# Activation tables set for single steps at the start of a feed-forward stage, and the first weight conversion behind the first activations

## The chip, the cores and the metric

The kernel runs on one core of one Trainium2 chip. The time is the device time of one execution in microseconds (us); lower is better. Five engines work side by side, each through its own queue in order: TensorE (PE in the profile; its weight loads are PEld), VectorE (DVE), ScalarE (ACT), GpSimd (POOL) and SyncE (SP, which here only issues DMAs).

## The reference, cut to what matters

Three blocks follow each other: attention with a compressive memory, a dense feed-forward block, and a layer of eight experts with routing. The change is in the second:

```
h  = x @ w_in                      # 2304 x 512  by 512 x 2048
sp = log1p(exp(min(h, 20)))        # h itself where h > 20
g  = h * tanh(sp)                  # Mish
y  = g @ w_out                     # 2304 x 2048 by 2048 x 512
```

The third block routes by the largest logit of y, so the kernel keeps products near full precision: each operand is split into a high part, rounded to the fp32r type of the matmuls, and the rest, and three products (high x high, low x high, high x low) are summed.

## The kernel before, in words

The tokens are cut into 9 blocks of 256 (`NBLK`), the 2048 hidden columns into 8 pairs of 128 (`STEPS`). A step is one block and one pair; there are 72, and `order` lists them: the first blocks 0 and 1 by turns, then block after block. So step 0 is block 0, pair 0; step 1 is block 1, pair 0; step 2 is block 0, pair 1.

For a step s there are these functions, and no planner: in this stage the order in which the program emits instructions is the order of every queue.

- `gemm1(s)`: 24 matmuls into a PSUM tile `ph`, of which there are three, so `gemm1(s + 3)` waits until ACT has read the tile of s.
- `mish_a(s)`: on ACT, Silu into g (L209) and a Tanh into t (L210). They belong to one activation table (`SILU`).
- `mish_b(s)`: Mish is finished with Arctan (L220) and Sin (L221), which lie in another table (`TRIG`). It does nothing for an even step; for an odd step it changes the table (L217), does Arctan and Sin for the steps s - 1 and s, and changes back (L222). DVE then does one operation per step (L225), `g = (t + c) * g`.
- `mish_d(s)`: splits g for the second product: on DVE a cast to gh (L232) and a subtraction to gl (L235).
- `gemm2(s)`: 12 matmuls that add the step into the sums `py` (L249 to L251). They read gh, gl and the steps' rows of `w_out`, both parts. Of three matmuls the first two read gh, the third gl.
- `convert(s)`: `w_out` arrives as float64 words and is converted while the first 16 steps run. A call does the high part of row block s on ACT (L834, tile u), the low part on POOL (L837), three bit operations for row block s + 1 on DVE (L813, L818, L824, which `cv.bits` issues), one load by SP (L792), and the scaling of row block s + 2 on ACT (L805). The high part of s needs the bit operations of s, issued by the call before.

The loop over s (L598) emits: `gemm1(s)`, `mish_a(s)`, `mish_d(s - 2)`, `mish_b(s)`, `convert(s + 1)` while there are rows left, and `gemm2(s - 3)` from s = 3 on. `convert(0)` stands ahead of the loop, with the bit operations of row block 1 in it; the bit operations of row block 0 are done during attention. `xs.load(2)` at s = 0 loads a block of tokens that attention stored.

The converted `w_out` tiles u lie in memory that attention used, so the first write to them waits until attention has ended, its last product on POOL (L1146) included. The tiles g, t, gh and gl are in other pools, opened later, in memory that attention's input tiles used.

Of the kernel before, what the change touches and what calls it, by code (L numbers as in the profile page):

```python
# [43 lines left out]
def fused_kernel(ctx, tc, qk, qn, vx, beta, w_in, w_out, wgs, wgk, w1, w2, out, dbg=None):  # L44
# [26 lines left out]
    more = ctx.enter_context(tc.tile_pool(name="more", bufs=1))  # L71
    uw += [more.tile([128, 4096], F32R, name=f"u{i}") for i in range(4, 8)]
    moe(tc, wgs, wgk, w1, w2, out, yd, rt, ident, shift, right, uw, xs, cv)
    if "xd" in dbg:
        for b in range(B):
# [33 lines left out]
def moe(tc, wgs, wgk, w1, w2, out, yd, rt, ident, shift, right, uw, xs, cv):  # L109
# [5 lines left out]
    with ExitStack() as ctx:  # L115
# [22 lines left out]
        def wo_parts(f):  # L138
            sl = slice((f % 8) * 512, (f % 8 + 1) * 512)
            return uw[4 + f // 8][:, sl], uw[6 + f // 8][:, sl]  # L140
# [17 lines left out]
        def tables():  # L158
            SP.dma_start(out=wgt, in_=wgk)
            G.iota(c8, [[-1, NE]], base=NE, channel_multiplier=0, allow_small_or_imprecise_dtypes=True)  # L160
            G.iota(tok, [[128, NTILE]], base=0, channel_multiplier=1)
            G.iota(spread, [[0, 1]], base=0, channel_multiplier=16, allow_small_or_imprecise_dtypes=True)
            V.memset(ones, 1.0)
            G.affine_select(out=tri, in_=ones, pattern=[[1, 128]], compare_op=ALU.is_gt, fill=0.0, base=0, channel_multiplier=-1)
            V.memset(cum, 0.0)
            V.memset(empty[:, :, 0:1], OOB)
            V.memset(empty[:, :, 1:2], 0)
            for e in range(NE):
                for t in range(2):
                    SP.dma_start(out=rtv[t][:, e], in_=empty)  # L170
            SP.dma_start(out=yd[N:N + 1, :].rearrange("a (p c) -> (a p) c", p=128), in_=ident[:, 0:4])

        def rows():
            for e in range(NE + 1):
                if e % 2 == 0 and e < 6:
                    pair = cv.pool.tile([128, 2, DM], F32, name="raw", bufs=cv.bufs[0])
                if e < 6:
                    row = pair[:, e % 2]
                else:
                    row = cv.pool.tile([128, DM], F32, name="cvt" if e < 8 else "cvf", bufs=2)  # L180
                SP.dma_start(out=row, in_=wgs[e:e + 1].to_broadcast([128, DM]))
                wrows.append(row)
            wrows.append(cv.pool.tile([128, DM], F32, name="cvf", bufs=2))
# [28 lines left out]

        def mish_b(s):

            if s % 2 == 0:
                return
            nc.scalar.preload_act_table_set(TRIG)  # L217
            for x in (s - 1, s):
                g, t = gs[x]
                A.activation(out=t, in_=t, func=AF.Arctan, scale=TAN8)  # L220
                A.activation(out=t, in_=t, func=AF.Sin, scale=2.0, bias=right)  # L221
            nc.scalar.preload_act_table_set(SILU)  # L222
            for x in (s - 1, s):
                g, t = gs[x]
                V.scalar_tensor_tensor(out=g, in0=t, scalar=ROOT_HALF, in1=g, op0=ALU.add, op1=ALU.mult)  # L225

        def mish_d(s):
            g, t = gs[s]
            gh = gp.tile([128, 2, TOK], F32R, name="gh")
            gl = gp.tile([128, 2, TOK], F32R, name="gl")  # L230
            if s < KF:
                V.tensor_copy(out=gh, in_=g)  # L232
            else:
                A.activation(out=gh, in_=g, func=AF.Copy)  # L234
            V.tensor_tensor(out=gl, in0=g, in1=gh.bitcast(F32), op=ALU.subtract)  # L235
            gs[s] = (gh, gl)
# [198 lines left out]
        def load_w(q=SP):  # L435
            tag = next((x for x in room if room[x]), None)
            if at[0] >= stop[0] or tag is None:
                return
            room[tag] -= 1
            r, m, c = chunks[at[0]]  # L440
            at[0] += 1
            rows = slice(c * 128 * (m + 1), (c + 1) * 128 * (m + 1))
            src = (w1, w2)[m][bass.ds(first_e[0], 1) if r == 0 else slice(r - 1, r), rows].rearrange("a p f -> (a p) f")
            pool = cv.pool if tag == "raw" else xs.pool
            raw = pool.tile([128, KD, TOK], F32, name=tag, bufs=size[tag]).rearrange("p a b -> p (a b)")
            if m == 0:
                q.dma_start(out=raw, in_=src)
            else:
                q.dma_start(out=raw.rearrange("p (k f) -> p k f", k=2),
                            in_=src.rearrange("(k p) f -> p k f", p=128))  # L450
            raws[r, m, c] = (raw, tag)
# [122 lines left out]
        def first_block(b):  # L574
            return stages(0, (ga, gb)[b]["first"], (ta, tb)[b]["first"], id0[:, b, 0:1], id0[:, b, 1:2].bitcast(F32))
# [6 lines left out]
        def convert(s):  # L582
            if s < KF:
                cv.high(s, *wo_parts(s))
                cv.low(s, *wo_parts(s))
            if s + 1 < KF:
                cv.bits(s + 1)
            if s + cv.ahead < KF:
                cv.load_out(s + cv.ahead)
            if s + 2 < KF:  # L590
                cv.scale(s + 2)

        def on(f, s):
            if 0 <= s < total:
                f(s)

        convert(0)
        for s in range(total + GLAG):  # L598
            i, j = order[s] if s < total else (NBLK, s - total)
            if s == 0:  # L600
                xs.load(2)
            if 2 <= i < NBLK - 1 and j == 0:
                xs.load(i + 1)
            on(gemm1, s)
            on(mish_a, s)
            on(mish_d, s - 2)
            on(mish_b, s)
            if s == 2 * STEPS - 2:
                for k in range(KD):
                    xs.split(2, k)  # L610
            if s + 1 < KF:
                convert(s + 1)
            if s == KF - 1:
                rows()
            if s == 6:
                tables()
            if 2 <= i < NBLK - 1 and 3 <= j < 3 + KD:
                xs.split(i + 1, j - 3)
            if s == total - STEPS:
                for _ in range(3):  # L620
                    load_w()
            if s == total - STEPS + 3:
                room["raw"] = 3
                for _ in range(3):
                    load_w()
            if s >= GLAG:
                b, jb = order[s - GLAG]
                gemm2(s - GLAG)
                if jb == STEPS - 1:
                    for n in (2 * b, 2 * b + 1):  # L630
                        store_y(n)
                if s == total:
                    first = first_block(0)
                    next(first)
                    first_gather(1)
                for q in tail_splits.get(s, ()):
                    split_w(q)
                if jb == STEPS - 1:
                    if b < NBLK - 1:
                        two_b = (2 * b, 2 * b + 1)  # L640
                        if b < 2 or b == NBLK - 2:
                            group = [[(logits, n) for n in two_b], [(logits2, n) for n in two_b], [(route_a, b)]]
                            if b == NBLK - 2:
                                for g, f in zip(group, ((fill_first,), (), (first_gather,))):
                                    g[:0] = [f] * bool(f)
                            todo += [[]] * (b == 0) + group
                        else:
                            flat = [(logit, n, e) for n in two_b for e in range(NE + 1)]
                            group = [flat[x:x + 3] for x in range(0, len(flat), 3)]
                            if b == NBLK - 3:  # L650
                                group[0][:0] = [(pick_first,)]
                            todo += group + [[(route_a, b)]]
                        if b == NBLK - 2:
                            todo += [[(turn_a, "first")], [(route_b, b)], [(route_c, b)]]
                        else:
                            todo += [[(route_b, b)], [(route_c, b)]]
            last = None
            while todo and (last is None or last is logit and todo[0][0][0] is route_a):
                last = 0
                for it in todo.pop(0):  # L660
                    it[0](*it[1:])
                    last = it[0]
# [177 lines left out]
class Work:  # L840
# [59 lines left out]
    on = {}  # L900
# [415 lines left out]
```

## Time and profile before

| | |
|---|---|
| median of three runs | 899.84 us (898.0 to 900.85) |
| the profiled execution | 903.65 us, its span 901.9 us |
| PE busy | 844.4 us, 94% of the span |
| ACT busy | 622.4 us, 69% |
| DVE busy | 577.8 us, 64% |
| POOL busy | 278.4 us, 31% |
| mean granted clock of TensorE | 0.978 of full speed |

The stage of the change begins at 235.26 us of the span, with the first matmul of `gemm1(0)`. Times in the rows below are counted from the span's start. In a timeline a row is one instruction: start, duration, engine, line, operation, what it writes and reads, and in brackets how long the engine sat idle before it and what ended that.

### The profile page before, as it was taken

The numbers are of one execution on the slowest core, as the hardware profiler recorded it, in microseconds if no ns is written. First come the engines' busy times: TensorE is split into PE (matmuls) and PEld (weight loads), VectorE is DVE, ScalarE is ACT, GpSimd is POOL, SyncE is SP. The second block draws the span as 40 slices with busy tenths as digits, with TensorE's granted clock in tenths as the row PEclk, the third lists the DMA queues.
The fourth block names the chain that finished last, engine by engine and source line by source line (L and its number), as shares of the span: only waits on it lengthen the run. The fifth ranks groups of instructions, "written<-read, shape, count | busy, mean of one in ns | idle before, by whom it ended". The sixth has DMA issues, their size and how long they took to land.

```text
span 901.9 us, 15116 instructions
## 1 busy us (share of the span) xinstructions
PE 844.4 (94%) x5412; PEld 687.3 (76%) x5412; DVE 577.8 (64%) x1171; ACT 622.4 (69%) x1136; POOL 278.4 (31%) x358
## 2 busy tenths in 40 slices
PE   5899999999889999999999999999988989989995
PEld 3566656666779998989898989888866867768774
DVE  6988878766488843356575757575558666373661
ACT  4687768876588887787878788787845555363551
POOL 5876776854223230110111111011103212211200
PEclk8999999999999999999999999999989999999998
DMA  6666657642333231010101010122336958284610
GB/s 211 192 197 206 200 168 230 214 143 87 123 94 110 94 129 49 24 47 24 48 24 48 25 48 24 48 94 95 95 125 211 349 197 288 67 288 151 198 62 4
DMA packets 53704, 113.44 MB, mean 126 GB/s; under 512 B 12148, under 2 KB 17396, under 8 KB 53600
## 3 DMA queue, kind: packets, MB, share of 16 engines
q1 hardware_dynamic: 43968, 91.22, 31.3%
q0 software_dynamic: 4064, 10.42, 3.5%
q10 hardware_dynamic: 5568, 10.49, 3.2%
q8 instruction: 56, 0.92, 0.4%
q14 instruction: 48, 0.39, 0.1%
HBM read 94.47 MB, written 18.77 MB: 126 GB/s over the span
## 4 chain that ended last, share of the span: by engine, by line
PE 40%; DMA 21%; issue 15%; ACT 8%; POOL 7%; DVE 5%; SPq 1%; ACTq 0%; POOLq 0%; another core or an unknown queue 0%; DVEq 0%
DMA cvt<-yd,ids 8%; DMA out<-cvf,ids 6%; PE ph L197 6%; PE ph L199 6%; PE ph L198 6%; PE py L249 6%; PE py L251 6%; PE py L250 6%; DMA r<-rd 3%; DMA qn<-qn 2%; PE px L1134 2%; PE pt L1106 2%; POOL mn L1027 1%; ACT e L1074 1%; DVE nm L1063 1%
## 5 line engine op out<-in xcount | busy, mean ns | idle before, releaser
L197 PE MATMUL ph<-xh,u 128*128 128x256 f32 x576 | 163.8, 284 | 0.9 <-DVE xr L1006 0.9
L199 PE MATMUL ph<-xh,u 128*128 128x256 f32 x576 | 162.5, 282 | 0.0
L198 PE MATMUL ph<-xl,u 128*128 128x256 f32 x576 | 162.3, 282 | 0.0
L249 PE MATMUL py<-u,gh 128*128 128x512 f32 x288 | 115.8, 402 | 4.9 <-POOL u L837 4.9
L251 PE MATMUL py<-u,gl 128*128 128x512 f32 x288 | 115.7, 402 | 4.2 <-DVE gl L235 4.2
L250 PE MATMUL py<-u,gh 128*128 128x512 f32 x288 | 115.1, 400 | 0.0
L197 PEld LDWEIGHTS ph<-xh,u 128*128 128x128 f32 x576 | 109.8, 191 | 3.4 <-DVE xr L1006 1.1
L198 PEld LDWEIGHTS ph<-xl,u 128*128 128x128 f32 x576 | 109.8, 191 | 2.5
L199 PEld LDWEIGHTS ph<-xh,u 128*128 128x128 f32 x576 | 109.8, 191 | 0.0
L225 DVE SCALAR_TENSOR_TENSOR g<-t,g 128x512 f32<-128x512 f32 x72 | 49.9, 693 | 92.0 <-ACT t L221 89.8
L1074 ACT ACTIVATE e<-ps,nm 128x256 f32<-128x256 f32 (+4 forms) x144 | 78.0, 550 | 29.7 <-DVE nm L1063 21.9
L235 DVE TENSOR_TENSOR gl<-g,gh 128x512 fp32r<-128x512 f32 x72 | 51.1, 709 | 62.4 <-ACT gh L234 53.9
L1106 PE MATMUL pt<-ident,e 128*128 128x128 f32 x528 | 77.0, 285 | 8.3 <-ACT eta L1008 5.6
L351 POOL DMA_INDIRECT rt<-pay,sl x18 | 22.1, 1225 | 181.6 <-DVE pay L349 178.8
L209 ACT ACTIVATE g<-ph 128x512 f32<-128x512 f32 x72 | 42.7, 593 | 46.8 <-PE ph L199 45.8
L1106 PEld LDWEIGHTS pt<-ident,e 128*128 128x128 f32 x528 | 57.5, 143 | 18.6 <-ACT eta L1008 7.5
L251 PEld LDWEIGHTS py<-u,gl 128*128 128x128 f32 x288 | 54.9, 191 | 19.5 <-DVE gl L235 6.3
L249 PEld LDWEIGHTS py<-u,gh 128*128 128x128 f32 x288 | 55.2, 192 | 15.6 <-POOL u L837 5.0
L106 POOL TENSOR_TENSOR xl<-xr,xh 128x256 fp32r<-128x256 f32 x36 | 31.5, 880 | 112.0 <-ACT xh L105 111.8
L837 POOL TENSOR_TENSOR u<-cvf,u 128x512 fp32r<-128x512 f32 x32 | 46.6, 1458 | 58.6 <-ACT u L834 58.6
L250 PEld LDWEIGHTS py<-u,gh 128*128 128x128 f32 x288 | 54.9, 191 | 9.9
L1063 DVE TENSOR_REDUCE nm<-ps 128x2 f32<-128x256 f32 (+1 forms) x64 | 51.1, 816 | 7.0 <-PE ps L1054 6.1
(236 smaller groups left out, 1976.7 us busy)
## 6 DMA issues: line engine op xcount, KB each, us to landing
raw<-w SPq DMA_DIRECT2D x26, 512.0 KB
qk<-qk SPq DMA_DIRECT2D x16, 608.0 KB
raw<-w_in SPq DMA_DIRECT2D x16, 512.0 KB
raw<-w_out SPq DMA_DIRECT2D x16, 512.0 KB
xl<-w SPq DMA_DIRECT2D x16, 512.0 KB
xh<-w SPq DMA_DIRECT2D x15, 512.0 KB
qn<-qn SPq DMA_DIRECT2D x16, 384.0 KB
vx<-vx SPq DMA_DIRECT2D x16, 320.0 KB
```

Source lines behind the costliest of these rows:

```text
L197: T.matmul(ps[:, f2], win(HI, k, f), hi[:, k], start=(k == 0), stop=False)
L198: T.matmul(ps[:, f2], win(HI, k, f), lo[:, k], start=False, stop=False)
L199: T.matmul(ps[:, f2], win(LO, k, f), hi[:, k], start=False, stop=(k == KD - 1))
L225: V.scalar_tensor_tensor(out=g, in0=t, scalar=ROOT_HALF, in1=g, op0=ALU.add, op1=ALU.mult)
L235: V.tensor_tensor(out=gl, in0=g, in1=gh.bitcast(F32), op=ALU.subtract)
L249: T.matmul(ys[i][t], gh[:, f2, ts], wout(HI, f), start=(f == 0), stop=False)
L250: T.matmul(ys[i][t], gh[:, f2, ts], wout(LO, f), start=False, stop=False)
L251: T.matmul(ys[i][t], gl[:, f2, ts], wout(HI, f), start=False, stop=(f == KF - 1))
L837: self.nc.gpsimd.tensor_tensor(out=lo, in0=self.now.pop(i), in1=hi.bitcast(F32), op=ALU.subtract)
L1063: V.tensor_reduce(out=nm, in_=ps[:, :, o:o + w], axis=AX.X, op=ALU.max, negate=True)
L1074: A.activation(out=E[p % 2][:, k, 64:64 + w], in_=src, func=AF.Exp, bias=nm[:, h:h + 1], scale=1.0, accum_out=SS[p % 2][:, 0, k:k + 1])
L1106: T.transpose(ps[:, c], E[p % 2][:, k, j * 128:(j + 1) * 128], ident)
```

## The change

For the steps 0 and 1, `mish_b` changes the table for that step alone, does its Arctan and Sin, and changes back; `mish_d` of these steps follows at once instead of two steps later. From step 2 on the pairs are as before. `convert(0)` moves from ahead of the loop to behind the first step's `mish_d`, with all that it issues; `convert(1)` follows it.

```diff
         def mish_b(s):
-            if s % 2 == 0:
+            if s and s % 2 == 0:
                 return
+            batch = (s,) if s < 2 else (s - 1, s)
             nc.scalar.preload_act_table_set(TRIG)
-            for x in (s - 1, s):
+            for x in batch:
                 g, t = gs[x]
                 A.activation(out=t, in_=t, func=AF.Arctan, scale=TAN8)
                 A.activation(out=t, in_=t, func=AF.Sin, scale=2.0, bias=right)
             nc.scalar.preload_act_table_set(SILU)
-            for x in (s - 1, s):
+            for x in batch:
                 g, t = gs[x]
                 V.scalar_tensor_tensor(out=g, in0=t, scalar=ROOT_HALF, in1=g, op0=ALU.add, op1=ALU.mult)
...
-        convert(0)
         for s in range(total + GLAG):
...
             on(gemm1, s)
             on(mish_a, s)
-            on(mish_d, s - 2)
+            if s > 3:
+                on(mish_d, s - 2)
             on(mish_b, s)
+            if s < 2:
+                mish_d(s)
+            if s == 0:
+                convert(0)
```

## Rows read from the trace of the kernel before

**Rows 1.** Busy time by stretch; columns: span, engines' busy us (instructions), PE clock, DMA share, GB/s

```profile
246.86:251.87 5.01, 0.16 (x2) 0.03 (x1) 4.33 (x7) 4.95 (x9) 1.62 (x1) 0.94 0.24 66
251.87:256.02 4.15, 4.15 (x12) 3.27 (x13) 4.05 (x6) 4.09 (x7) 1.63 (x1) 0.66 0.25 71
267.34:640.00 372.66, 371.79 (x2412) 334.84 (x2411) 221.52 (x574) 299.25 (x449) 60.64 (x58) 1.00 0.18 59
```

**Rows 2.** Timeline of PE, 235 to 268 us: where products of steps begin or end

```profile
238.10 0.28 PE L199 MATMUL ph<-xh,u 128*128 128x256 f32 x1
...
246.74 0.28 PE L199 MATMUL ph<-xh,u 128*128 128x256 f32 x1
251.87 0.77 PE L249 MATMUL py<-u,gh 128*128 128x512 f32 x1 [4.86 <-POOL u L837]
...
264.54 0.40 PE L249 MATMUL py<-u,gh 128*128 128x512 f32 x1
...
267.34 0.28 PE L197 MATMUL ph<-xh,u 128*128 128x256 f32 x1
```

**Rows 3.** Timeline of ACT, 239 to 257 us

```profile
239.45 0.63 ACT L834 ACTIVATE u<-cvf 128x512 fp32r<-128x512 f32 x1 [6.76 <-POOL xr L1146]
...
240.55 0.58 ACT L209 ACTIVATE g<-ph 128x512 f32<-128x512 f32 x1
...
241.60 0.64 ACT L834 ACTIVATE u<-cvf 128x512 fp32r<-128x512 f32 x1
...
242.68 0.61 ACT L209 ACTIVATE g<-ph 128x512 f32<-128x512 f32 x1
243.16 0.71 ACT L210 ACTIVATE t<-ph,shift 128x512 f32<-128x512 f32 x1
243.89 1.28 ACT L217 ACT_TABLE_LOAD   x1
...
245.85 0.72 ACT L221 ACTIVATE t<-t,right 128x512 f32<-128x512 f32 x1
...
247.13 0.72 ACT L221 ACTIVATE t<-t,right 128x512 f32<-128x512 f32 x1
247.87 1.28 ACT L222 ACT_TABLE_LOAD   x1
...
256.82 0.72 ACT L221 ACTIVATE t<-t,right 128x512 f32<-128x512 f32 x1
```

**Rows 4.** Timeline of DVE, 235 to 262 us

```profile
235.12 0.42 DVE L813 TENSOR_SCALAR cvf<-cvt 128x512 int32<-128x512 int32 x1
...
242.69 1.67 DVE L824 SCALAR_TENSOR_TENSOR cvf<-cvt,cvf 128x512 int32<-128x512 int32 x1
...
255.29 0.42 DVE L232 CAST gh<-g 128x512 fp32r<-128x512 f32 x1
255.75 0.69 DVE L235 TENSOR_TENSOR gl<-g,gh 128x512 fp32r<-128x512 f32 x1
256.35 0.69 DVE L225 SCALAR_TENSOR_TENSOR g<-t,g 128x512 f32<-128x512 f32 x1
257.57 0.69 DVE L225 SCALAR_TENSOR_TENSOR g<-t,g 128x512 f32<-128x512 f32 x1 [0.54 <-ACT t L221]
258.19 0.42 DVE L813 TENSOR_SCALAR cvf<-cvt 128x512 int32<-128x512 int32 x1
258.64 0.69 DVE L818 SCALAR_TENSOR_TENSOR cvf<-raw,cvf 128x512 int32<-128x512 int32 x1
...
259.98 1.52 DVE L232 CAST gh<-g 128x512 fp32r<-128x512 f32 x1
```

**Rows 5.** Timeline of POOL, the low part at 242 us

```profile
242.31 1.50 POOL L837 TENSOR_TENSOR u<-cvf,u 128x512 fp32r<-128x512 f32 x1 [0.85 <-ACT u L834]
```

**Rows 6.** Timeline during attention, 16 to 20 us: one instruction of POOL and one of DVE

```profile
17.82 1.27 POOL L1027 TENSOR_TENSOR mn<-qn 128x512 f32<-128x512 f32 x1
...
17.99 1.64 DVE L818 SCALAR_TENSOR_TENSOR cvf<-raw,cvf 128x512 int32<-128x512 int32 x1
```

## The prediction, made before the changed kernel was run

> **What bounds the kernel now.** I read the table of stretches first, then the timelines of PE, ACT and DVE from the start of the feed-forward stage, and last the instructions that POOL and DVE run at the same time. From 267.34 to 640 us PE is busy for 371.79 of 372.66 us at full clock, ACT for 299.25 and DVE for 221.52 [rows 1]. So PE has no slack there: what is lost or won before 267.34 is carried to the end, and a late ACT or DVE catches up. Only the start of the stage is open. A step of `gemm1` takes 2.88 us, a third of the way from the last matmul of step 0 at 238.10 to that of step 3 at 246.74; `gemm2` takes 2.80 us at full clock, from 264.54 to 267.34 [rows 2]. PE is through with `gemm1(3)` at 246.86, one matmul pitch behind that last start, and stands still until 251.87, when `gemm2(0)` begins. Then TensorE's granted clock is 0.66 on average, so part of the twelve matmuls run at the half-speed level (1.2 of 2.4 GHz), and they take 4.15 us instead of 2.80 [rows 1]. The change aims at these 5.01 + 1.35 = 6.4 us. They come from ACT, which starts only at 239.45 with a conversion and then works without a gap through both first steps before Sin and the table come [rows 3].
>
> **The first step in the new order.** ACT begins with Silu 0. `gemm1(0)` ends at 238.10 + 0.28 [rows 2], so at 238.4. From a Silu to the table load are 1.21 us (242.68 to 243.89), on to the Sin 1.96 (to 245.85), from a Sin to the load back 0.74 (247.13 to 247.87), and that load takes 1.28 [rows 3]. Sin 0 is at 241.6, and the conversion's high part 0 at 243.6. On DVE the product L225 starts 0.75 after the Sin (256.82 [rows 3], 257.57 [rows 4]); the next operation is 0.62 later, a cast is followed by the subtraction after 0.46, and that by the next after 0.60 [rows 4]. So the cast is at 242.9, the subtraction from 243.4 to 244.1. The low part 0 is asked of POOL 0.71 after the high part (241.60 [rows 3], 242.31 [rows 5]), at 244.3, and is through at 245.8. All that `gemm2(0)` reads is there when PE comes at 246.86, with 1 us to spare. **The first stall goes**, its slow matmuls with it.
>
> **What moves with `convert(0)`.** The bit operations of row block 1 ran at 235.12, in DVE's idle time [rows 4]. Now they stand behind the subtraction: L813 at 244.0, L818 0.45 later at 244.45. POOL has its low part since 244.3. The trace shows what happens then: L824 began at 242.69 while POOL worked from 242.31 to 243.81, and ended at 244.36, 1.67 long and 0.55 behind POOL's end [rows 4, 5]; L818 itself, begun at 17.99 while L1027 ran from 17.82 to 19.09, ended at 19.63 [rows 6]. Undisturbed it takes 0.69 [rows 4]. So L818 ends at 245.81 + 0.55 = 246.36, L824 at 247.1, and the high part 1 on ACT waits for it. ACT could have gone on 1.10 after the high part 0 (239.45 to 240.55 [rows 3]), at 244.7: a new wait of 2.4 us. Its bounds are 1.2 (no hold: the three operations take 1.79 to the next start, 258.19 to 259.98 [rows 4], and the last of them 0.08 more) and 2.4; I take 2.4, since L818 has a row of its own.
>
> SP now issues `xs.load(2)` ahead of the load of row block 4. The first waits for attention's store as before and is not read before step 14: nothing. The second waits for L818 and goes out at 246.4; its data are wanted at about 253.9, 7.5 us later. At the stretch's 66 GB/s [rows 1] half a megabyte needs 7.9 us, and 0.4 would still fall into a wait named below. Price 0.
>
> **The second step.** High part 1 at 247.1, Silu 1 1.08 later (241.60 to 242.68 [rows 3]) at 248.2, table load at 249.4, Sin 1 at 251.35, load back at 252.1, high part 2 at 253.4. The Tanh is through just ahead of 249.4, so `gemm1(4)` has its PSUM tile when `gemm2(0)` ends at 246.86 + 2.80 = 249.7, and runs to 252.5. The cast of step 1 ends at 253.1, the subtraction at 253.9: PE waits 0.6 for gh and 0.25 at the third matmul for gl. `gemm2(1)` ends at 256.2, `gemm1(5)` at 259.1. On DVE the bit operations of row block 3 meet the low part 2 as before: L813 at 253.8, POOL from 254.1 to 255.6, L824 through at 256.9. ACT, free for high part 3 at 253.4 + 2.15 = 255.5 (239.45 to 241.60 [rows 3]), waits another 1.4 us (bounds 0.15 and 1.4).
>
> **The pair of steps 2 and 3 is late.** High part 3 at 256.9, Silu 3 at 258.0, table load at 259.2, Sin 2 at 261.15, Sin 3 1.28 later (245.85 to 247.13 [rows 3]) at 262.4. Before, that Sin was at 256.82: ACT starts 1.05 sooner, has two more table loads with their gaps, 2.9, and waits 3.8 for DVE, 5.6 later in all. DVE then does the product of step 3 and the bit operations of row block 5 ahead of the cast of step 2, which POOL holds; the cast ended 3.93 behind the product's start (257.57 to 261.50 [rows 4]). So gh of step 2 is there at 267.1, and PE, free since 259.1, begins `gemm2(2)` at 267.15 instead of 264.54 [rows 2]: 2.6 late, behind a stall of 8 us, longer than the one removed. Behind the 5.01 us the clock fell; I let it cost the same 1.35 here (bounds 0 and 2.80, twelve matmuls all at half speed). `gemm1(6)` begins 2.6 + 1.35 = 4.0 us later than before.
>
> After that nothing is late: `gemm2(3)` comes at 274.2, and the subtraction, the three bit operations with one hold and the next cast and subtraction end by 273. The sum is **+4.0 us** on the profiled 903.65; that run lies 0.4% above the median of the runs, to which I add the same 4.0.
>
> **A rule weighed.** A table load lies between a Tanh that ends at 243.87 and an Arctan inside the 1.96 us to the Sin; it starts at 243.89 and no gap surrounds it [rows 3]. The Trainium skill ("ScalarE: Activation LUTs", section "What ACT_TABLE_LOAD costs") puts 1.28 us for the load and about 1.38 for a drain, 2.66 for a switch. By that page the two added loads would cost some 2.8 us more, and the change would lose near 7. The trace disagrees with the drain; I go by its spacing.
>
> **The rivals.**
> 1. POOL gives way and DVE is never held. Place: L818 behind low part 0, and the same behind low parts 2 and 4. The waits shrink to 1.2 and 0.15, Sin 3 is at 260.0, and the cast of step 2 ends at 260.8 + 0.62 + 1.79 + 0.42 = 263.6. PE starts 0.9 sooner than before, the clock costs 1.35: +0.5, not slower by what can be told. If the cast alone is still held, as at 259.98 for 1.52 us [rows 4], +1.6. It decides at L818: 0.69 or about 1.9 us. Against it: rows 4 to 6.
> 2. Silu 0 also waits for attention's last product on POOL, as the high part did until 239.45 [rows 3]. For it: a new pool's tile may wait for old ones; against it: g lies over attention's inputs, not over what that product reads. All of ACT comes 1.05 later: +5.0.
> 3. The clean gain: the first stall goes and `gemm2(2)` finds gh when PE comes at 259.1. That is -6.4 + 0.85 = -5.5 us. It needs Sin 3 at 254.4; ACT's own durations without any wait give 258.7.
> 4. ACT pauses at each of the two added loads for as long again as the load takes, 1.28 us [rows 3]: 2.6 us more, +6.6. No load in the rows has such a gap beside it. (The page weighed above would have it so.)
>
> **How the numbers follow.** The forecast has 66%, with a range of its own of +2.8 to +5.0. Rival 1 has 14%, rival 2 10%, rival 3 3%, rival 4 1%; 6% are for what I don't see, close to no change. A measurement tells 0.3%, 2.7 us, from no change. Slower: nearly all of the forecast, rivals 2 and 4, 74%. Same: rival 1, the forecast's low end and most of the rest, 22%. Faster: 4%. The time is 899.84 + 4.0 = 903.8. The range goes from +1.2, inside rival 1, to +5.8, which holds rival 2 and a longer slow stretch: 901.0 to 905.6.
>
> **What would show it.** In the changed kernel's PE timeline `gemm2(0)` follows `gemm1(3)` without a gap at about 246.9, and `gemm2(2)` begins behind an idle time of 7 to 8 us, at about 267, at half clock. L818 takes 1.5 to 1.9 us there and ACT is idle for 2.4 and 1.4 us ahead of two L834. ACT's first Silu is at 238.4. I'm wrong in kind if `gemm2(2)` begins before 264, and in size if ACT's two waits are near 1.2 and 0, or if the stall leaves the clock up.

## The result and the profile after

The changed kernel is slower: 907.92 us against 900.9 (medians of 12 runs each), ratio 1.0061, interval 1.0035 to 1.0086. By the ratio that is +5.5 us, by the two medians +7.0. Two more series of it, beside the experiments, gave 1.0037 (1.0016 to 1.0058) and 1.0040 (1.0017 to 1.0063), with medians of 905.67 and 905.24. The forecast was +4.0 us, a ratio of 1.0044, and 903.8 us. The sign came out, and all three intervals contain the ratio; the first median lies 2.3 us above the top of the range, 905.6.

The profiled execution took 902.67 us (span 901.0), less than that of the kernel before; so totals of single profiles say nothing here, and the stage has to be looked at. I take the **stage time**: from the first matmul of `gemm1(0)` to the first of `gemm1(6)`. It was 267.34 - 235.26 = 32.08 us before [rows 2]. The timeline of PE in the changed kernel:

```profile
232.90 0.39 PE L197 MATMUL ph<-xh,u 128*128 128x256 f32 x1 [0.86 <-DVE xr L1011]
...
244.50 0.40 PE L250 MATMUL py<-u,gh 128*128 128x512 f32 x1
...
247.05 0.50 PE L251 MATMUL py<-u,gh 128*128 128x512 f32 x1 [0.76 <-POOL u L842]
...
264.71 0.79 PE L250 MATMUL py<-u,gh 128*128 128x512 f32 x1 [7.48 <-DVE gh L233]
...
269.69 0.28 PE L197 MATMUL ph<-xh,u 128*128 128x256 f32 x1
```

The stage begins 2.36 us earlier in this execution, so times count from 232.90. `gemm2(0)` comes at 11.60, where it stood still until 16.61 before: the first stall is gone. `gemm2(2)` comes at 31.81 behind an idle time of 7.48 us, 29.28 before: the stall has moved and grown. The stage ends at 36.79, 4.71 later than before. The stretches of that stall and of `gemm2(2)`, cut 0.25 us ahead of its first matmul, and of all that follows to 640 us (columns as in rows 1):

```profile
256.98:264.46 7.48, 0.26 (x3) 0.05 (x1) 4.58 (x7) 7.38 (x11) 1.62 (x1) 0.87 0.26 84
264.46:269.69 5.23, 4.97 (x13) 3.82 (x13) 4.95 (x8) 5.15 (x8) 1.70 (x1) 0.54 0.37 114
269.69:640.00 370.31, 369.29 (x2399) 332.73 (x2398) 220.64 (x571) 295.56 (x442) 60.62 (x58) 1.00 0.18 58
```

The granted clock is 0.54 in `gemm2(2)`; behind it PE is as busy as before [rows 1]. What made the pair late is in the timeline of ACT:

```profile
236.19 0.60 ACT L209 ACTIVATE g<-ph 128x512 f32<-128x512 f32 x1 [5.85 <-PE ph L199]
236.69 0.68 ACT L210 ACTIVATE t<-ph,shift 128x512 f32<-128x512 f32 x1
237.38 1.28 ACT L218 ACT_TABLE_LOAD   x1
238.68 0.63 ACT L221 ACTIVATE t<-t 128x512 f32<-128x512 f32 x1
...
241.38 0.63 ACT L839 ACTIVATE u<-cvf 128x512 fp32r<-128x512 f32 x1
...
244.83 0.63 ACT L839 ACTIVATE u<-cvf 128x512 fp32r<-128x512 f32 x1 [2.25 <-DVE cvf L829]
...
254.51 0.63 ACT L839 ACTIVATE u<-cvf 128x512 fp32r<-128x512 f32 x1 [1.13 <-DVE cvf L829]
...
260.02 0.72 ACT L222 ACTIVATE t<-t,right 128x512 f32<-128x512 f32 x1
```

ACT starts with Silu 0, 3.29 behind the first matmul, when `gemm1(0)` is through; then the two waits, 2.25 and 1.13 us, each ended by DVE's last bit operation. Sin 3 is at 27.12, where it was at 21.56 (256.82 - 235.26 [rows 2, 3]): 5.6 later. DVE and POOL at those two waits, and the cast of step 2:

```profile
242.41 1.67 DVE L823 SCALAR_TENSOR_TENSOR cvf<-raw,cvf 128x512 int32<-128x512 int32 x1
...
252.09 1.67 DVE L823 SCALAR_TENSOR_TENSOR cvf<-raw,cvf 128x512 int32<-128x512 int32 x1
...
263.17 1.49 DVE L233 CAST gh<-g 128x512 fp32r<-128x512 f32 x1
```

```profile
242.09 1.44 POOL L842 TENSOR_TENSOR u<-cvf,u 128x512 fp32r<-128x512 f32 x1 [5.06 <-ACT u L839]
245.54 1.46 POOL L842 TENSOR_TENSOR u<-cvf,u 128x512 fp32r<-128x512 f32 x1 [2.01 <-ACT u L839]
251.82 1.38 POOL L842 TENSOR_TENSOR u<-cvf,u 128x512 fp32r<-128x512 f32 x1 [4.83 <-ACT u L839]
```

L823 (L818 before) takes 1.67 instead of 0.69 us [rows 4]; POOL's low part begins ahead of it both times, at 242.09 and 251.82, and L823 ends 0.5 to 0.6 behind POOL.

### The profile page after: what moved, and what is told of

It is laid out like the page before. It is cut to its first block, busy times and chain, and to the rows that moved or that the text cites. A ratio compares the mean times of both kernels' runs of the same rounds, so it can differ in the third digit from the quotient of the medians.

```text
span 901.0 us, 15119 instructions
## 1 busy us (share of the span) xinstructions
PE 839.9 (93%) x5412; PEld 683.8 (76%) x5412; DVE 581.2 (65%) x1171; ACT 625.1 (69%) x1138; POOL 279.3 (31%) x358
```

## The experiments

All are compared with the kernel before on the same chip; a stage "before" of 32.08 us is that of its first profile. e1, e2, e4 and e6 are edits of the changed kernel, e3, e7 and e8 of the kernel before. The first matmul of `gemm1(0)` is the zero of the times quoted.

**e1: the bit operations of row block 1 back in DVE's idle time.**

```diff
 def convert(s):
...
-            if s + 1 < KF:
+            if s + 1 < KF and s:
                 cv.bits(s + 1)
...
+        cv.bits(1)
         for s in range(total + GLAG):
```

> The changed kernel, but the three bit operations of row block 1 stay ahead of the loop, where DVE is idle. Stage time = first matmul of gemm1(0) to first matmul of gemm1(6): 32.08 us in the kernel before, 36.79 in the changed one. Theory (two added table loads and two waits of ACT for DVE make the pair 2, 3 late): ACT's wait of 2.25 us ahead of the high part 1 goes, the other of 1.1 to 1.4 stays; Sin 3 comes 25 us after the first matmul instead of 27.1, gemm2(2) 29.5 instead of 31.8, stage 34.4, total near +2.4 us against before. Rival (the waits are covered, the added table loads alone make it late): Sin 3 and stage as in the changed kernel, 36.8.

Ratio 1.0004 (0.998 to 1.0027). The first wait of ACT is gone, the second is there:

```profile
252.94 0.63 ACT L840 ACTIVATE u<-cvf 128x512 fp32r<-128x512 f32 x1 [1.13 <-DVE cvf L830]
...
258.46 0.72 ACT L222 ACTIVATE t<-t,right 128x512 f32<-128x512 f32 x1
```

```profile
263.15 0.80 PE L250 MATMUL py<-u,gh 128*128 128x512 f32 x1 [6.36 <-DVE gh L233]
...
268.05 0.28 PE L197 MATMUL ph<-xh,u 128*128 128x256 f32 x1
```

With the first matmul at 233.70, Sin 3 is at 24.76 and `gemm2(2)` at 29.45; the stage takes 34.35 (34.4 expected). So 2.4 of the 4.7 us come from moving three DVE instructions with `convert(0)`. The ratio, +0.4 us, is below the +2.4 expected, which is its upper end; see e9.

**e2: the tables for single steps alone**, `convert(0)` ahead of the loop as before.

```diff
+        convert(0)
         for s in range(total + GLAG):
...
-            if s == 0:
-                convert(0)
```

> The first part of the change alone: tables for the single steps 0 and 1, and convert(0) ahead of the loop as before. Theory: ACT starts with the high part 0 at 4.2 us after the first matmul, has no wait for the bit operations of row block 1, and waits 1.3 us for those of row block 3; gemm2(0) follows gemm1(3) without a stall, Sin 3 at 25.8, gemm2(2) at 30.5 behind a stall of over 7 us, its matmuls slow; stage 35.5, total +3.4 us. Rival (the move of convert(0) is what costs): stage no longer than before, 32.1, total 0 or a gain.

Ratio 1.0028 (1.0004 to 1.0053). PE's timeline, and ACT's Sin 3:

```profile
235.70 0.39 PE L197 MATMUL ph<-xh,u 128*128 128x256 f32 x1 [0.86 <-DVE xr L1010]
...
247.31 0.40 PE L250 MATMUL py<-u,gh 128*128 128x512 f32 x1
...
266.18 0.80 PE L250 MATMUL py<-u,gh 128*128 128x512 f32 x1 [7.40 <-DVE gh L233]
...
270.73 0.28 PE L197 MATMUL ph<-xh,u 128*128 128x256 f32 x1
```

```profile
261.49 0.72 ACT L222 ACTIVATE t<-t,right 128x512 f32<-128x512 f32 x1
```

No first stall, Sin 3 at 25.79 as expected, `gemm2(2)` at 30.48, the stage 35.03 (35.5 expected): the single tables move the stall by themselves and cost 3 us against 32.08. e1 and e2 differ only in where the rest of `convert(0)` stands; ACT's earlier start in e1 gives 0.7 us back (34.35 against 35.03). So 3.0 for the tables, less 0.7 for the start, and 2.4 for the moved bit operations make up the 4.7.

**e3: the move of `convert(0)` alone**, from the kernel before.

```diff
-        convert(0)
         for s in range(total + GLAG):
...
             on(mish_a, s)
+            if s == 0:
+                convert(0)
             on(mish_d, s - 2)
```

> The second part alone: convert(0) behind the Silu and Tanh of step 0, tables in pairs as before; the bit operations of row block 1 are still the first on DVE. Theory: ACT starts 1.0 us sooner and the first stall is shorter by that, 3.9 instead of 4.9 us; no wait of ACT for DVE; stage 31.1 to 31.2, total -0.9 us. Rival (Silu 0 waits for attention's last product too, or convert's place costs): stage 32.1 or more.

Ratio 0.9989 (0.9966 to 1.0012): no difference that can be told. In the trace the stall is shorter by the 0.9 us expected, and the twelve matmuls behind it are slower (4.44 us against 4.15 [rows 1]), so the stage is 31.48:

```profile
233.68 0.39 PE L197 MATMUL ph<-xh,u 128*128 128x256 f32 x1 [0.86 <-DVE xr L1007]
...
249.38 0.57 PE L249 MATMUL py<-u,gh 128*128 128x512 f32 x1 [3.92 <-ACT t L210]
...
265.16 0.28 PE L197 MATMUL ph<-xh,u 128*128 128x256 f32 x1
```

Without the single tables nothing stands ahead of the bit operations of row block 1 on DVE, so ACT has no wait for them and the move gains ACT's earlier start.

**e4: what the clock costs.** 28 matmuls without use ahead of `gemm2(2)`.

```diff
+                if s == GLAG + 2:
+                    warm = pp.tile([128, 512], F32, name="pr", bufs=1)
+                    for _ in range(28):
+                        T.matmul(warm, xs.parts[0][1][:, 0, 0:128], uw[0][:, 0:512], start=True, stop=True)
```

> The changed kernel with 28 extra matmuls of 128x512 (6.6 us at full clock) ahead of gemm2(2), in the time in which PE stands still for 7.5 us; their sum is not used. It measures what the slow clock behind the stall costs. Theory: gemm2(2) begins when gh is there, as in the changed kernel (31.8 after the first matmul), and takes 2.8 us instead of 5.0: stage 34.6, total +2.5 us. Rival (the matmuls of gemm2(2) were slow for another cause, or the clock falls anyway): stage 36.8.

Ratio 1.0011 (0.9992 to 1.0031). The clock stays at 1.00, in the stretch filled with the extra matmuls and in `gemm2(2)`, which takes 3.22 us instead of 4.98; it begins at 31.83, as in the changed kernel:

```profile
259.12:266.78 7.66, 6.54 (x31) 5.08 (x29) 4.70 (x7) 7.55 (x12) 1.62 (x1) 1.00 0.32 105
266.78:270.00 3.22, 3.16 (x12) 2.28 (x13) 3.10 (x4) 3.19 (x6) 1.72 (x1) 1.00 0.17 70
```

The stage is 35.05, 1.74 shorter than in the changed kernel (2.2 expected: 0.4 are left, of them some 0.2 for gl, which is ready later than PE wants it at full clock).

**e6: no low part on POOL while DVE does the bit operations of row blocks 1 and 3.**

```diff
-                cv.low(s, *wo_parts(s))
+                if s not in (0, 2):
+                    cv.low(s, *wo_parts(s))
             if s + 1 < KF:
                 cv.bits(s + 1)
+            if s in (0, 2):
+                cv.low(s, *wo_parts(s), V)
```

> The changed kernel with the low parts of row blocks 0 and 2 on DVE, behind the bit operations, instead of on POOL; so POOL is idle while the bit operations of row blocks 1 and 3 run. Theory (half of each of ACT's two waits is DVE held by POOL): L823 there takes 0.69 us instead of 1.67, ACT waits 1.2 instead of 2.25 and 0.15 instead of 1.13 us, Sin 3 comes at 25.1 after the first matmul instead of 27.1, stage 34.7 instead of 36.8. Rival (the operations are long for themselves, because of their place behind the cast): L823 stays at 1.67, Sin 3 at 27.1, stage 36.8.

Ratio 0.9995 (0.9976 to 1.0015). The two instructions of DVE and the two waits of ACT:

```profile
244.20 0.69 DVE L826 SCALAR_TENSOR_TENSOR cvf<-raw,cvf 128x512 int32<-128x512 int32 x1
...
252.88 0.69 DVE L826 SCALAR_TENSOR_TENSOR cvf<-raw,cvf 128x512 int32<-128x512 int32 x1
```

```profile
245.65 0.63 ACT L842 ACTIVATE u<-cvf 128x512 fp32r<-128x512 f32 x1 [1.28 <-DVE cvf L832]
...
254.33 0.63 ACT L842 ACTIVATE u<-cvf 128x512 fp32r<-128x512 f32 x1 [0.16 <-DVE cvf L832]
...
259.84 0.72 ACT L222 ACTIVATE t<-t,right 128x512 f32<-128x512 f32 x1
```

0.69 us each, waits of 1.28 and 0.16 (1.2 and 0.15 expected), Sin 3 at 25.17 (first matmul at 234.67), stage 34.37 (34.7 expected). POOL held DVE, shown by taking POOL away: 1 us in each wait. The Trainium skill says why ("SBUF — State Buffer", section "Who interferes with whom"): an operation of VectorE with two inputs in SBUF shares a port pair with a GpSimd instruction that reads SBUF, and whichever comes first keeps it. The trace agrees: 1.67 us against 0.69.

**e7 and e8: the conversions in ACT's gap, without a further table load.** From the kernel before, `convert(0)` moves as in e3; `mish_d` follows at once; the bit operations of row block 3 go ahead. e7 does that for steps 0 and 1:

```diff
 def mish_b(s):
...
                 V.scalar_tensor_tensor(out=g, in0=t, scalar=ROOT_HALF, in1=g, op0=ALU.add, op1=ALU.mult)
+                if s == 1:
+                    mish_d(x)
...
-            if s + 1 < KF:
+            if s + 1 < KF and s != 2:
                 cv.bits(s + 1)
...
-        convert(0)
         for s in range(total + GLAG):
...
             on(mish_a, s)
-            on(mish_d, s - 2)
+            if s == 0:
+                convert(0)
+            if s > 3:
+                on(mish_d, s - 2)
+            if s == 1:
+                cv.bits(3)
             on(mish_b, s)
```

e8 does it also for the even step of every later pair of the first 16 (`if s < KF and (x < s or s == 1): mish_d(x)`, the odd ones as before), with `gemm2(s - GLAG)` emitted ahead of `mish_b(s)` there.

> The kernel before, pairs for all tables, with convert(0) behind the Silu and Tanh of step 0, mish_d of steps 0 and 1 at once behind their products on DVE, and the bit operations of row block 3 ahead of them; nothing else. Theory (ACT has the time between the first two gemm1 for the conversions, and gh of step 0 was late because DVE was held): gh of step 0 at 11.5 us after the first matmul, no first stall; gemm2(2) still waits for its cast, which follows the bit operations of row block 5 and the held cast, until 25.4: a stall of 2.3, stage 28.2, total -3.9 us. Rival (the pair's table loads put gh of step 0 later than gemm1(3) whatever the order): a first stall of 2 us or more, stage 30 or more.

> As e7, and for every pair of the first 16 steps the cast and subtraction of the even step at once behind its product, ahead of the odd step's product and the bit operations; gemm2 is emitted ahead of mish_b there, which leaves PE's order as it is. Theory: gh of step 2 is ready at 21.2 us, PE needs it at 23.1: no stall at all, stage 25.9 instead of 32.1, total -6.2 us (0.7%). Rival (ACT or the conversions become the bound of the later pairs): the stage gains but PE stalls in steps 4 to 15, total -3 us or less.

e7: ratio 0.9927 (0.990 to 0.9954), median 897.04 us, five runs, stage 28.60 (28.2 expected). Its timelines of PE, ACT (Sin 0) and DVE (cast of step 0):

```profile
235.02 0.39 PE L197 MATMUL ph<-xh,u 128*128 128x256 f32 x1 [0.86 <-DVE xr L1012]
...
247.35 0.47 PE L251 MATMUL py<-u,gh 128*128 128x512 f32 x1 [0.55 <-issue]
...
260.38 0.50 PE L251 MATMUL py<-u,gh 128*128 128x512 f32 x1 [1.23 <-DVE gh L234]
...
263.62 0.28 PE L197 MATMUL ph<-xh,u 128*128 128x256 f32 x1
```

```profile
244.70 0.73 ACT L221 ACTIVATE t<-t,right 128x512 f32<-128x512 f32 x1
```

```profile
246.82 0.43 DVE L234 CAST gh<-g 128x512 fp32r<-128x512 f32 x1
```

`gemm2(0)` begins at 12.33, behind 0.55 us without work (none expected), and `gemm2(2)` at 25.36 as expected, behind 1.23 (2.3 expected). e3 and e7 differ only in DVE's order. Sin 0 is at 9.67 and 9.68, `gemm2(0)` at 15.70 and 12.33: DVE's order by itself is worth 3.4 us of the first stall.

e8: ratio 0.9908 (0.988 to 0.9937), median 895.95 us, six runs, stage 27.06 (25.9 expected):

```profile
235.55 0.38 PE L197 MATMUL ph<-xh,u 128*128 128x256 f32 x1 [0.86 <-DVE xr L1015]
...
262.61 0.28 PE L197 MATMUL ph<-xh,u 128*128 128x256 f32 x1
```

The waits of PE in e8, from the stage's start to 640 us (what waited, for whom, us, times, longest):

```profile
PE ph L197 <- DVE xr L1015: 0.9, 1, 0.9
PE py L251 <- ACT t L221: 0.8, 1, 0.8
PE py L253 <- DVE gl L237: 0.4, 1, 0.4
```

No stall of several us is left, so e8's rival falls. The 0.8 weren't expected: the bit operations of row blocks 2 and 3 stand ahead of the first product on DVE, begin only behind POOL's low part 0 and are held by low part 1, so gh of step 0 is 1 us late. The first of these operations:

```profile
242.25 1.50 DVE L822 TENSOR_SCALAR cvf<-cvt 128x512 int32<-128x512 int32 x1 [4.97 <-POOL u L846]
```

Both ratios (-6.6 and -8.3 us) are some 3 us better than the stage gives against 32.08 (-3.5 and -5.0), and the intervals don't reach these numbers; e9 bears on it.

**e5, e9, e10: the two kernels again**, to tell the change from the spread.

> The changed kernel once more, unaltered, beside the experiments. Theory (all that the change does lies between the first matmul of gemm1(0) and that of gemm1(6), where it costs 4.7 us): total +4 to +5.5 us against before, stage 36.8. Rival (the change also costs some 2 us elsewhere, which a first difference of the medians of 7 us hints at): total +6 us or more, with attention or the experts longer than in the profiles of the other kernels.

> The kernel before, unaltered, timed as if it were an experiment: how far two series of one kernel differ, and a second profile of it. Theory (attention and the experts, which no kernel here touches, vary from run to run by some us): ratio 1.000 with an interval of 0.002 to each side, stage 32.1; attention up to the first gemm1 and the part behind the last gemm1 anywhere in the range of the nine other profiles (232.9 to 235.7 and 231.3 to 233.9 us). Rival (the order of the kernel before makes its later parts longer): the part behind the last gemm1 above 234 us again.

> The changed kernel for the third time, beside the copy of the kernel before. Theory: ratio 1.004 to 1.0055, as the stage's 4.7 to 5.0 us say. Rival (another 2 us elsewhere): 1.006 or more.

The ratios of the changed kernel are above: 1.0037 (e5) and 1.0040 (e10). For e5 that is +3.3 us, under its theory's +4 to +5.5 and far from the rival's +6. The copy of the kernel before has 1.000 (0.9978 to 1.0022). Its stage was 33.29 us, not 32.1: attention's last product on POOL held ACT's first conversion until 4.68 behind the first matmul (4.19 in the first profile [rows 3]), the stall was 5.33 us, and then came `gemm2(0)`, in the last row here; the first two are `gemm2(2)` in e5 and e10:

```profile
265.97:271.25 5.28, 5.28 (x12) 4.03 (x13) 5.06 (x7) 5.18 (x9) 1.69 (x1) 0.50 0.35 120
266.92:271.35 4.43, 4.43 (x12) 3.43 (x13) 4.21 (x6) 4.37 (x8) 1.68 (x1) 0.62 0.27 74
251.47:256.31 4.84, 4.84 (x12) 3.77 (x13) 4.74 (x7) 4.78 (x8) 1.63 (x1) 0.55 0.30 97
```

The three profiles of the changed kernel have 36.79, 37.10 and 36.28, those of the kernel before 32.08 and 33.29: 36.7 - 32.7 = 4.0 us, by few profiles. The ratios suggest that 32.08 is short for the kernel before: in all ten series from e1 to e10 they lie below what the stage gives against 32.08, by 0.4 to 3.3 us, and against 33.29 they lie on both sides, from 2.1 below to 0.8 above, with e7's and e8's intervals reaching the stage's number. That is argued from two profiles, not shown. In all twelve profiles the part up to the first `gemm1` took 232.9 to 235.7 us and that from the last `gemm1` to the experts' last first-layer matmul 230.1 to 234.7, in no order that goes with the change. The rival for e9 falls: that part was 231.2 there, 234.7 in the first profile. For e10, 1.0040 is the theory's lower end.

## Why the prediction was right or wrong

**The mechanism of the new order held step by step.** The first stall goes (`gemm2(0)` without a gap). ACT starts with Silu 0 at 3.29 us, so rival 2 fell. L823 is held, 1.67 us, and ACT waits 2.25 us (2.4 forecast): rival 1 fell, and e6 shows the hold to be POOL's. The second wait was 1.13 (1.4 forecast). Sin 3 came 5.6 us late, as forecast, and `gemm2(2)` 2.53 late (2.6 forecast). e1 and e2 give the shares: 2.4 us for the bit operations that moved with `convert(0)`, 3 us for the single tables by themselves, less 0.7 for ACT's earlier start. Rival 3, the clean gain, fell by the 7.48 us stall; a load still begins where the Tanh ends (237.37) and is followed by the Arctan 0.02 us behind its end, so rival 4 fell.

Part of the close match is luck. `gemm2(2)` came at 31.81, 31.82 and 31.85 in the three profiles of the changed kernel, but in those of the kernel before at 29.28 and 30.49: against the second it is 1.4 late, not 2.5.

**The premise named the wrong engine for most of the first stall.** The prediction says that the stall comes from ACT. In the kernel before, Sin 0 began at 10.59 (245.85 [rows 3]), and the cast of step 0 ended at 16.51, just ahead of `gemm2(0)`:

```profile
250.28 1.49 DVE L232 CAST gh<-g 128x512 fp32r<-128x512 f32 x1
```

The cast stood behind both products and three bit operations on DVE, and took 1.49 us instead of 0.42. With DVE's order changed and the tables in pairs (e7 against e3) 3.4 us of the stall go; ACT's earlier start by itself (e3) is worth 0.9. The forecast doesn't hang on this, since the change brings that order too, but the single tables weren't needed for it.

**The clock term was too small.** I let the second stall cost the 1.35 us of the first. `gemm2(2)` took 4.98, 5.28 and 4.43 us in three profiles of the changed kernel, 1.6 to 2.5 more than at full clock, with 2.18 in the first; e4, with the clock up, gave 1.74 of that back. Behind the shorter stall of the kernel before it was 1.35 in one profile and 2.0 in the other. A single row was taken for a constant.

**One read was missed.** The first stall's end was put to gh, gl and row block 0. `gemm2(0)` reads row blocks 0 and 1, and waited 0.76 us for low part 1, which ended on POOL at 247.00 (245.54 and 1.46), made late by the same wait of ACT. The later stall swallowed it.

**The step that failed is the base, the clock term and a spread put at nothing.** The forecast adds 4.0 to the median of three runs, 899.84, and its range is built from the bounds of the stage's costs alone. It missed the first median, 907.92, by 4.1 us. Of these 1.1 are the base: twelve runs of the kernel before had a median of 900.9, and later series up to 902.42. Another 0.7 are the stage (4.71 instead of 4.0): the clock term alone, 2.18 instead of 1.35, is 0.8 more. The other 2.3 aren't in the stage as profiled, and their cause stays open. I named 0.3%, 2.7 us, as what a measurement can tell, but gave what executions of one kernel differ by no place in the range. The same changed kernel had medians of 907.92, 905.67 and 905.24, and in the twelve profiles the parts ahead of the stage and behind it vary by 2.8 and 4.6 us. No profile shows one of the first series' long runs: the one profiled is its shortest. Within that series the four shortest runs (902.67 to 905.34) have a mean granted clock of 0.981 to 0.986, the other eight (907.46 to 911.9) 0.975 to 0.982; but the mean over the series is 0.980 in all three, so this doesn't tell them apart. That the first series was high by chance is suggested by the two later ones, +3.3 and +3.6 us, and not proved.

## What to carry to other kernels

Before moving work to end a stall, follow the data that ends it back through every engine: here the cast that `gemm2(0)` waited for was late more by DVE's order than by ACT. Giving the engine with the long queue more work sooner moved the stall; add up its queue to the products behind the first as well. When a function moves, look at every queue it feeds; three vector instructions that had run in an idle stretch cost half of the loss here. Reordering DVE's work and filling ACT's own gap (e8) shortened the stage by 5.0 us against 32.08, most of the 6.4 that the change was after. A forecast of a total needs a base and a spread from more than three runs.

## What the runs showed of the hardware that I had not expected

The same twelve matmuls behind a stall took very different times, in no clear order with the length of the stall:

| run | PE idle ahead, us | twelve matmuls, us |
|---|---|---|
| e3 | 3.92 | 4.44 |
| before | 4.86 | 4.15 |
| e9 (the same kernel) | 5.33 | 4.84 |
| e1 | 6.36 | 4.90 |
| e6 | 6.51 | 4.50 |
| e2 | 7.40 | 4.55 |
| e5 (the changed kernel) | 7.47 | 5.28 |
| after | 7.48 | 4.98 |
| e10 (the changed kernel) | 7.50 | 4.43 |

At the full clock level they take 2.80 us and start 0.23 us apart. Behind the stalls they start 0.43 us apart at first, from six of them (before) to all twelve (e5), with a granted clock of 0.66 to 0.50 over the stretch. With extra matmuls in the stall (e4) the granted clock stayed at 1.00 and they took 3.22.
